# Linear attention with a two-layer SMELU feed-forward: loads put in an order, and scores, intra part and state moved to zero-padded weights

## The chip, the cores and the metric

The kernel runs on one core of one Trainium2 chip. The metric is the device time of one execution in microseconds (us). Several executions of each kernel are timed in the same rounds on the same chip, and each is marked fast or slow; only fast ones are compared. A profile's "span" is the time from its first to its last instruction. It is somewhat shorter than the reported time: 286.2 us against 287.86 us in the profiled execution of the changed kernel.

Engines are named as in the profile: PE is the matrix engine and PEld its weight load, DVE the vector engine, ACT the scalar engine, POOL the third elementwise engine (it also issues the weight loads here), SP the engine that issues most other transfers.

## The reference, cut to what matters

```python
# q, k, v: (4, 8, 768, 64) fp32, lam: (8,); w_in: (512, 2048), w_out: (2048, 512)
for b in range(nb):                                    # blocks of the sequence
    intra = einsum('bhic,bhjc->bhij', qb, kb) * Dmask  # lam^(i-j), lower triangle
    intra = einsum('bhij,bhjd->bhid', intra, vb)
    inter = einsum('bhid,bhde->bhie', qb * lam_pow, kv_state)
    out[:, :, sl] = intra + inter
    kv_state = lam_block * kv_state + einsum('bhsd,bhse->bhde', kb * rev_pow, vb)
x = out.transpose(0, 2, 1, 3).reshape(3072, 512)
h = x @ w_in
g = where(h >= 1, h, where(h <= -1, 0, (h + 1) ** 2 / 4))
return g @ w_out                                       # (3072, 512) fp32
```

The kernel cuts the 3072 tokens into 24 chunks of 128 (6 per batch entry). A chunk is done in two *units* of four heads, so there are 48 units. Four chunks make a *tile* of 512 tokens for the feed-forward layers; there are 6 tiles.

## The kernel before: the parts that matter

Each unit has three stages. `t` transposes q and multiplies k with [v | identity], which gives the state's update and k^T at once. `s` makes the scores, `o` the output of the chunk.

```python
def cast(c, k_eng):                      # fp32 to bf16, times lam^(+-position)
    nc.gpsimd.tensor_tensor(qs, qf, tab_q, mult)       # POOL
    k_eng.tensor_tensor(ks, kf, tab_k, mult)           # DVE for chunks 0-3, then POOL
    nc.scalar.copy(out=vi[c % NV][:, :, 0, :], in_=vf) # ACT; vi = [v | identity]

def stage_t(u):
    # 2 x transpose(pq <- qs), 2 x matmul(pk <- ks as weights, vi as rhs: 256 columns)
    for hi in range(2):
        nc.scalar.copy(out=qbd[u % NQ][hi*64:hi*64+64, :, hi, :], in_=pq[hi*64:hi*64+64])
    nc.scalar.copy(out=kT, in_=pk[:, :, 1, :])
    # U = pk[:, :, 0, :] + U of the chunk before                      (DVE)

def stage_s(u):
    for j in range(2):                   # q is block-diagonal and MOVES: 256 columns
        nc.tensor.matmul(ps[:, 2*j:2*j+2, :], lhsT=kT[:, j, :], rhs=qbd[u % NQ][:, j])
    # sc = ps * causal                                                (DVE)

def stage_o(u):
    for j in range(2):                   # 256 columns each
        # if not the first chunk: po[:, j] += U x qbd
        nc.tensor.matmul(po[:, j], lhsT=vi[..., hp, 0, :], rhs=sc[:, 2*j:2*j+2, :])
    # two ACT copies of 64 partitions put the diagonal blocks of po into xT

def att(i):                              # the order of the attention steps
    u, odd = i // 2, i % 2
    if not odd: ...                      # stage_t(u), and behind it stage_o(u - 1)
    else: ...                            # stage_s(u)
```

The order of the program is the order on each engine:

```python
load(0); load(1) ...                     # q, k, v of a chunk, 256 KB each
for c in range(4):                       # chunks 0 to 3
    cast(c)
    if c >= 1: load_w_in(...)            # weights between the chunks
    # four steps: t(2c), o(2c-1), s(2c), t(2c+1), o(2c), s(2c+1)
load_w_in(...); 4 x load_w_out(...)
ensure_cast(4); # one step: t(8), o(7)
for s in range(NST + 1):                 # then every group of layer 1 and layer 2
    for i in range(FO):                  # has an attention step woven into it
        ensure_loaded(c + 5); ensure_cast(c + 1)
        l1(s, i); todo_a(); smelu(s, i); l2(s - 1, i); todo_b()
```

In layer 1, ACT makes `r` = relu(`ph` + 1), and DVE makes from it `t` = min(r/2, 1), `w` = r - t and `gT` = w x t, the activated input of layer 2.

So chunks 4 to 8 are already worked on during layer 1 of the first tile, and the casts of a chunk are issued one chunk ahead.

Of the kernel before, what the change touches and what calls it, by code (L numbers as in the profile page):

```python
# [23 lines left out]
def kernel(  # L24
# [30 lines left out]
    NU = NCH * 2  # L55

    const = ctx.enter_context(tc.tile_pool(name="const", bufs=1))
    big = ctx.enter_context(tc.tile_pool(name="big", bufs=1))
    ld = ctx.enter_context(tc.tile_pool(name="ld", bufs=6))
    qkp = ctx.enter_context(tc.tile_pool(name="qkp", bufs=3))  # L60
    ktp = ctx.enter_context(tc.tile_pool(name="ktp", bufs=3))
    scp = ctx.enter_context(tc.tile_pool(name="scp", bufs=2))
    up = ctx.enter_context(tc.tile_pool(name="up", bufs=3))
# [15 lines left out]
    qkv_ld = {}  # L79

    def load(c):
        b, s0 = c // NCB, (c % NCB) * C
        ts = []
        for name, src in (("q", q), ("k", k), ("v", v)):
            t = ld.tile([128, H, D], F32, name=f"{name}f", tag=f"{name}f")
            nc.sync.dma_start(out=t, in_=src[b, :, s0:s0 + C, :].rearrange("h p d -> p h d"))
            ts.append(t)
        qkv_ld[c] = ts

    lam_b = const.tile([128, H], F32)  # L90
    nc.sync.dma_start(out=lam_b, in_=lam.partition_broadcast(128))
# [26 lines left out]
    NQ = 3  # L118
    qbd = []
    for i in range(NQ):  # L120
        t = const.tile([128, 2, 2, 128], BF16, name=f"qbd{i}")
        nc.vector.memset(t, 0.0)
        qbd.append(t)
    NV = 3
    vi = []
    for i in range(NV):
        t = const.tile([128, HP, 2, 128], BF16, name=f"vi{i}")
        nc.vector.tensor_copy(t[:, :, 1, :], _bc(ident, 1, HP))
        vi.append(t)

# [7 lines left out]
    def load_w_in(i):  # L138
        n = d_ff // WS
        nc.gpsimd.dma_start(out=w_in_sb[:, :, i * n:(i + 1) * n], in_=w_in_r[:, :, i * n:(i + 1) * n])  # L140

    def load_w_out(i):
        n = FO // WS
        nc.gpsimd.dma_start(out=w_out_sb[:, i * n:(i + 1) * n, :], in_=w_out_r[:, i * n:(i + 1) * n, :])
# [4 lines left out]
    def cast(c, k_eng):  # L149
        qf, kf, vf = qkv_ld.pop(c)  # L150
        cb = c % NCB
        t = qkp.tile([128, H, D], BF16, name="qs", tag="qs")
        nc.gpsimd.tensor_tensor(t, qf, _bc(tab_q[:, cb, :], 2, D), op=AX.mult)  # L153
        qs[c] = t
        t = qkp.tile([128, H, D], BF16, name="ks", tag="ks")
        k_eng.tensor_tensor(t, kf, _bc(tab_k[:, cb, :], 2, D), op=AX.mult)  # L156
        ks[c] = t
        nc.scalar.copy(out=vi[c % NV][:, :, 0, :], in_=vf.rearrange("p (a b) d -> p a (b d)", b=2))  # L158

    kT, U, sc_sb, xT = {}, {}, {}, {}  # L160

    def stage_t(u):
        c, hf = u // 2, u % 2
        cb = c % NCB
        pq = pp_q.tile([128, 2, 128], BF16, name="pq", tag="pq")
        pk = pp_k.tile([128, 2, 2, 128], F32, name="pk", tag="pk")
        for j in range(2):
            hp = 2 * hf + j
            nc.tensor.transpose(out=pq[:, j, :], in_=qs[c][:, 2 * hp:2 * hp + 2, :].rearrange("p a d -> p (a d)"),  # L169
                                identity=ident)  # L170
        for j in range(2):
            hp = 2 * hf + j
            nc.tensor.matmul(pk[:, j], lhsT=ks[c][:, 2 * hp:2 * hp + 2, :].rearrange("p a d -> p (a d)"),  # L173
                             rhs=vi[c % NV][:, hp], start=True, stop=True)
        qb = qbd[u % NQ]
        for hi in range(2):
            nc.scalar.copy(out=qb[hi * 64:hi * 64 + 64, :, hi, :], in_=pq[hi * 64:hi * 64 + 64])  # L177
        t = ktp.tile([128, 2, 128], BF16, name="kT", tag="kT")
        nc.scalar.copy(out=t, in_=pk[:, :, 1, :])  # L179
        kT[u] = t  # L180
        if cb < NCB - 1:
            t = up.tile([128, 2, 128], BF16, name="U", tag=f"U{hf}")
            if cb == 0:
                nc.vector.tensor_copy(t, pk[:, :, 0, :])
            else:
                nc.vector.tensor_tensor(t, pk[:, :, 0, :], U[u - 2], op=AX.add)  # L186
            U[u] = t

    def stage_s(u):
        ps = pp_s.tile([128, 4, 128], F32, name="ps", tag="ps")  # L190
        for j in range(2):
            nc.tensor.matmul(ps[:, 2 * j:2 * j + 2, :], lhsT=kT[u][:, j, :], rhs=qbd[u % NQ][:, j],  # L192
                             start=True, stop=True)
        t = scp.tile([128, 4, 128], BF16, name="sc", tag="sc")
        nc.vector.tensor_tensor(t, ps, _bc(causal, 1, 4), op=AX.mult)  # L195
        sc_sb[u] = t

    def stage_o(u):
        c, hf = u // 2, u % 2
        cb = c % NCB  # L200
        st, off = c // CPS, (c % CPS) * C
        po = pp_o.tile([128, 2, 2, 128], F32, name="po", tag="po")
        for j in range(2):
            hp = 2 * hf + j
            if cb > 0:
                nc.tensor.matmul(po[:, j], lhsT=U[u - 2][:, j, :], rhs=qbd[u % NQ][:, j], start=True, stop=False)  # L206
            nc.tensor.matmul(po[:, j], lhsT=vi[c % NV][:, hp, 0, :], rhs=sc_sb[u][:, 2 * j:2 * j + 2, :],  # L207
                             start=(cb == 0), stop=True)
        if st not in xT:
            xT[st] = xp.tile([128, KO, MS], BF16, name="xT", tag="xT")  # L210
        for hi in range(2):
            nc.scalar.copy(out=xT[st][hi * 64:hi * 64 + 64, 2 * hf:2 * hf + 2, off:off + C],  # L212
                           in_=po[hi * 64:hi * 64 + 64, :, hi, :])

    def att(i):

        u, odd = i // 2, i % 2
        a, b_ = [], []
        if not odd:
            if u < NU:  # L220
                a.append(lambda: stage_t(u))
            if 1 <= u <= NU:
                b_.append(lambda: stage_o(u - 1))
        elif u < NU:
            a.append(lambda: stage_s(u))
        return a, b_
# [4 lines left out]
    def l1(s, ni):  # L231
        ph = pp_h.tile([128, MS], F32, name="ph", tag="ph")
        for ko in range(KO):
            nc.tensor.matmul(ph, lhsT=w_in_sb[:, ko, ni * 128:(ni + 1) * 128], rhs=xT[s][:, ko, :],  # L234
                             start=(ko == 0), stop=(ko == KO - 1))
        if ni % 2 == 0:
            r_t[s] = rp.tile([128, 2, MS], BF16, name="r", tag="r")
        nc.scalar.activation(out=r_t[s][:, ni % 2, :], in_=ph, func=AF.Relu, bias=one[:, 0:1])  # L238

    def smelu(s, ni):  # L240
        if ni % 2 == 0:
            return
        r = r_t[s]
        if ni == 1:
# [5 lines left out]
        nc.vector.tensor_tensor(gT[s][:, ni - 1:ni + 1, :], w, t, op=AX.mult)  # L250
# [16 lines left out]
    PF = 5  # L267
    state = {"ld": 2, "cast": 0, "att": 0, "wi": 0, "wo": 0}

    def ensure_loaded(c):  # L270
        while state["ld"] <= min(c, NCH - 1):
            load(state["ld"])
            state["ld"] += 1

    def ensure_cast(c, k_eng=None):
        while state["cast"] <= min(c, NCH - 1):
            cast(state["cast"], k_eng or nc.gpsimd)
            state["cast"] += 1

    def att_step():  # L280
        a, b_ = att(state["att"])
        state["att"] += 1
        return a, b_

    NSUB = 2 * NU + 1


    ensure_loaded(CPS - 1)
    for c in range(CPS):
        ensure_cast(c, nc.vector)  # L290
        if c >= 1:
            load_w_in(state["wi"])
            state["wi"] += 1
        for _ in range(4):
            a, b_ = att_step()
            for f in a + b_:
                f()
    load_w_in(state["wi"])
    for i in range(WS):
        load_w_out(i)  # L300
    ensure_loaded(CPS + 1)
    ensure_cast(CPS)
    a, b_ = att_step()
    for f in a + b_:
        f()
    ensure_loaded(CPS + PF)

    def target(g):

        base = 4 * CPS + 1  # L310
        if g < 16:
            return base + (18 * (g + 1)) // 16
        return min(NSUB, base + 18 + (g - 15))

    for s in range(NST + 1):
        for i in range(FO):
            g = s * FO + i
            todo_a, todo_b = [], []
            while state["att"] < min(NSUB, target(g)):
                c = state["att"] // 4  # L320
                ensure_loaded(c + PF)
                ensure_cast(c + 1)
                a, b_ = att_step()
                todo_a += a
                todo_b += b_
            if s < NST:
                l1(s, i)
            for f in todo_a:
                f()
            if s < NST:  # L330
                smelu(s, i)
            if s > 0:
                l2(s - 1, i)
            for f in todo_b:
                f()
# [30 lines left out]
```

## Time and profile before

| what | before | where it is read |
|---|---|---|
| time | 263.87 us median (263.35 to 264.07, 4 runs) | runs |
| first layer-1 matmul (`ph`) | 43.19 us | timeline |
| first layer-2 matmul (`py`) | 79.10 us | timeline |
| PE idle before the first `py` | 35.6 of 79.1 us | windows |
| PE idle after it | 5.1 of 184.4 us | windows |
| 512-column matmul at full clock | 0.217 us | timeline |

The windows view of the kernel before, cut at its first `py`. Columns: stretch, its length, then for each engine the busy time with the number of instructions, the granted PE clock, the DMA share and GB/s.

```profile
0.00:79.10 79.10, 43.49 (x234) 23.83 (x237) 40.58 (x68) 49.77 (x119) 29.36 (x37) 0.89 1.17 203
79.10:263.50 184.40, 179.31 (x978) 94.84 (x995) 103.21 (x178) 123.94 (x270) 24.87 (x24) 0.99 0.29 73
```

The first number after a comma is PE. After 79.1 us PE is busy nearly without a break: from there on only fewer or faster matmuls help. Before it, PE is idle for 35.6 us. (23 of the 1232 matmul records are missing from this trace, so these sums are a little low.) The waits of PE in the kernel before say on what (engine, line, releaser: us in total, times, longest):

```profile
PE pk L173 <- ACT vi_152 L158: 12.6, 1, 12.6
PE pq L169 <- POOL qs L153: 6.7, 1, 6.7
PE ps L192 <- ACT kT L179: 5.0, 8, 1.9
PE po L207 <- DVE sc L195: 2.6, 2, 2.4
```

The one long wait is for the v cast of chunk 4, and the page says that ACT waited for the load itself there (11.9 us).

The timeline of PE before, an ordinary unit at 120 us (start, length, engine, line, what; lines of DVE, PEld and others left out):

```profile
120.33 0.28 PE L169 MATMUL pq<-ident,qs 128*128 128x128 bf16 x2
120.44 0.38 PE L173 MATMUL pk<-vi_152,ks 128*128 128x256 bf16 x2
120.66 1.03 PE L258 MATMUL py<-w_out_sb,gT 128*128 128x512 bf16 x4
...
121.12 0.74 ACT L177 COPY qbd_144<-pq 64x256 bf16<-64x256 bf16 x2
...
121.89 0.37 ACT L179 CAST kT<-pk 128x256 bf16<-128x256 f32 x1
121.96 1.03 PE L234 MATMUL ph<-xT,w_in_sb 128*128 128x512 bf16 x4
...
122.83 0.38 PE L192 MATMUL ps<-qbd_144,kT 128*128 128x256 bf16 x2
```

Between `pk` and `ps` stand a `py` group, an `o` stage and a `ph` group. That is time for all three ACT copies; PE does not wait. Starts give the cost of the matmuls: the four `py` matmuls start at 120.66 and what follows them starts at 121.53, so 0.217 us each; the two transposes take 0.11 us, or 0.055 us each. The Trainium skill (TensorE: Matmul & The Clock Gate, "Wait — 56ns, not 53.3ns?") gives 215.7 and 55.6 ns for back-to-back matmuls of 512 and 128 columns at full clock, and this trace agrees.

### The profile page before, as it was taken

What the parts mean: (1) busy time and instruction counts of PE and PEld (TensorE: products, weight loads), DVE (VectorE), ACT (ScalarE), POOL (GpSimd) and SP (SyncE); (2) the same over time, 40 slices, a digit from 0 to 9 for tenths busy, and PEclk for the clock granted to TensorE, in tenths of its full rate; (3) what the DMA queues carried; (4) which work ended last, traced back from release to release, by engine and by line L of the source; (5) the groups of instructions that cost most, each with busy time, mean ns of one, the idle gap of its engine ahead of it and who ended that gap; (6) DMA issues with size and microseconds to landing.
All of it is one profiled execution on the core that took longest, in us unless ns stands there. A gap on an engine that the chain in (4) does not pass through costs nothing.

```text
span 263.5 us, 3576 instructions
## 1 busy us (share of the span) xinstructions
PE 222.8 (85%) x1209; PEld 118.7 (45%) x1232; DVE 143.8 (55%) x245; ACT 173.7 (66%) x389; POOL 54.2 (21%) x61
## 2 busy tenths in 40 slices
PE   0567306666889999999999999999999999999993
PEld 0234203333445555555555555555555544444441
DVE  3554201388887576657574766574747645555300
ACT  4768303778996977797779777977796754554210
POOL 3418111552340332033303320333000000000000
PEclk9999755999999999999999999999999999999998
DMA  6999999999990526753574357110111011111122
GB/s 134 210 217 187 196 196 220 210 226 218 218 202 2 138 67 120 159 128 85 108 159 121 88 113 163 40 40 0 42 41 40 2 40 40 40 42 40 40 80 80
DMA packets 82721, 29.58 MB, mean 112 GB/s; under 512 B 75536, under 2 KB 79632, under 8 KB 82704
## 3 DMA queue, kind: packets, MB, share of 16 engines
q1 hardware_dynamic: 78480, 25.18, 45.5%
q0 software_dynamic: 4224, 4.19, 9.7%
q8 instruction: 9, 0.15, 0.3%
q14 instruction: 8, 0.07, 0.1%
HBM read 27.27 MB, written 6.29 MB: 127 GB/s over the span
## 4 chain that ended last, share of the span: by engine, by line
PE 69%; DVE 3%; ACT 1%; issue 0%; ACTq 0%
PE py L258 31%; PE ph L234 26%; PE po L207 3%; PE ps L192 3%; PE pk L173 2%; PE po L206 2%; PE pq L169 1%; DVE gT L250 1%; DVE w_726 L249 1%; DVE sc L195 0%; DVE w_768 L249 0%; ACT r L238 0%; DVE U L186 0%; ACT xT L212 0%; ACT osb L262 0%
## 5 line engine op out<-in xcount | busy, mean ns | idle before, releaser
L234 PE MATMUL ph<-xT,w_in_sb 128*128 128x512 bf16 x380 | 99.6, 383 | 1.7 <-ACT r L238 1.3
L238 ACT ACTIVATE r<-ph,one 128x512 bf16<-128x512 f32 x96 | 65.9, 687 | 43.3 <-PE ph L234 39.6
L258 PE MATMUL py<-w_out_sb,gT 128*128 128x512 bf16 x365 | 92.3, 379 | 1.0
L234 PEld LDWEIGHTS <-w_in_sb 128*128 128x128 bf16 x384 | 37.9, 99 | 37.6 <-issue 2.8
L258 PEld LDWEIGHTS <-gT 128*128 128x128 bf16 x384 | 37.6, 98 | 32.3
L153 POOL TENSOR_TENSOR qs<-qf,tab_q 128x512 bf16<-128x512 f32 x24 | 25.3, 1052 | 121.7 <-PE pq L169 92.0
L186 DVE TENSOR_TENSOR U<-pk,U 128x256 bf16<-128x256 f32 x32 | 13.6, 424 | 56.5 <-ACT kT L179 56.5
L212 ACT CAST xT<-po 64x256 bf16<-64x256 f32 x96 | 35.3, 367 | 4.5 <-PE po L207 3.7
L195 DVE TENSOR_TENSOR sc<-ps,causal 128x512 bf16<-128x512 f32 x48 | 32.9, 685 | 4.6 <-PE ps L192 4.0
L156 POOL TENSOR_TENSOR ks<-kf,tab_k 128x512 bf16<-128x512 f32 x20 | 22.3, 1117 | 7.9 <-DMA kf<-in_k_dram 7.9
L262 ACT COPY osb<-py 128x512 f32<-128x512 f32 x24 | 14.2, 591 | 12.4 <-PE py L258 12.4
L169 PE MATMUL pq<-ident,qs 128*128 128x128 bf16 x96 | 14.3, 235 | 6.7 <-POOL qs L153 6.7
L179 ACT CAST kT<-pk 128x256 bf16<-128x256 f32 x48 | 17.9, 372 | 2.4 <-PE pk L173 1.3
L173 PE MATMUL pk<-vi_152,ks 128*128 128x256 bf16 x32 | 6.8, 298 | 14.6 <-ACT vi_152 L158 12.6
L169 PEld LDWEIGHTS <-qs 128*128 128x128 bf16 x96 | 10.1, 106 | 16.8 <-POOL qs L153 6.7
L173 PEld LDWEIGHTS <-ks 128*128 128x128 bf16 x96 | 8.1, 103 | 20.5 <-issue 8.1
L192 PEld LDWEIGHTS <-kT 128*128 128x128 bf16 x96 | 8.5, 101 | 19.4 <-ACT kT L179 11.0
L158 ACT CAST vi_152<-vf 128x512 bf16<-128x512 f32 x8 | 4.9, 610 | 11.9 <-DMA vf<-in_v_dram 11.9
L177 ACT COPY qbd_146<-pq 64x256 bf16<-64x256 bf16 x32 | 11.6, 361 | 1.6 <-PE pq L169 1.2
L177 ACT COPY qbd_144<-pq 64x256 bf16<-64x256 bf16 x32 | 11.5, 361 | 0.6 <-PE pq L169 0.2
L177 ACT COPY qbd_148<-pq 64x256 bf16<-64x256 bf16 x32 | 11.5, 361 | 0.5
L206 PEld LDWEIGHTS <-U 128*128 128x128 bf16 x80 | 8.2, 102 | 7.8 <-issue 3.7
(187 smaller groups left out, 213.9 us busy)
## 6 DMA issues: line engine op xcount, KB each, us to landing
qf<-in_q_dram SPq DMA_DIRECT2D x24, 256.0 KB, 4.8
kf<-in_k_dram SPq DMA_DIRECT2D x24, 256.0 KB, 4.7
vf<-in_v_dram SPq DMA_DIRECT2D x24, 256.0 KB, 5.0
out_dram<-osb SPq DMA_DIRECT2D x24, 256.0 KB, 2.0
w_in_sb<-in_moe_w_in_dram POOLq DMA_DIRECT2D x4, 512.0 KB, 8.7
w_out_sb<-in_moe_w_out_dram POOLq DMA_DIRECT2D x4, 512.0 KB, 15.5
lam_b<-in_lam_dram SPq DMA_DIRECT2D x1, 4.0 KB, 2.9
```

Source lines behind the costliest of these rows:

```text
L153: nc.gpsimd.tensor_tensor(t, qf, _bc(tab_q[:, cb, :], 2, D), op=AX.mult)
L156: k_eng.tensor_tensor(t, kf, _bc(tab_k[:, cb, :], 2, D), op=AX.mult)
L169: nc.tensor.transpose(out=pq[:, j, :], in_=qs[c][:, 2 * hp:2 * hp + 2, :].rearrange("p a d -> p (a d)"), identity=ident)
L173: nc.tensor.matmul(pk[:, j], lhsT=ks[c][:, 2 * hp:2 * hp + 2, :].rearrange("p a d -> p (a d)"), rhs=vi[c % NV][:, hp], start=True, stop=True)
L177: nc.scalar.copy(out=qb[hi * 64:hi * 64 + 64, :, hi, :], in_=pq[hi * 64:hi * 64 + 64])
L179: nc.scalar.copy(out=t, in_=pk[:, :, 1, :])
L192: nc.tensor.matmul(ps[:, 2 * j:2 * j + 2, :], lhsT=kT[u][:, j, :], rhs=qbd[u % NQ][:, j], start=True, stop=True)
L195: nc.vector.tensor_tensor(t, ps, _bc(causal, 1, 4), op=AX.mult)
L212: nc.scalar.copy(out=xT[st][hi * 64:hi * 64 + 64, 2 * hf:2 * hf + 2, off:off + C], in_=po[hi * 64:hi * 64 + 64, :, hi, :])
L234: nc.tensor.matmul(ph, lhsT=w_in_sb[:, ko, ni * 128:(ni + 1) * 128], rhs=xT[s][:, ko, :], start=(ko == 0), stop=(ko == KO - 1))
L238: nc.scalar.activation(out=r_t[s][:, ni % 2, :], in_=ph, func=AF.Relu, bias=one[:, 0:1])
L258: nc.tensor.matmul(py, lhsT=gT[s][:, ko, ms * 128:(ms + 1) * 128], rhs=w_out_sb[:, ko, :], start=(ko == 0), stop=(ko == FO - 1))
```

## The change

The intent is twofold.

*Form.* Instead of moving a half-empty block-diagonal q (256 columns), k^T and v are made zero-padded *weights*, and q^T moves as it is (128 columns). In `s` four full-array matmuls of 128 columns replace two of 256. In `o` the state matmul moves 128 columns instead of 256, and the intra matmuls accumulate both heads into one output, so one ACT copy replaces two. The state is kept in block-diagonal tiles of 128 columns. The padding must be cleared once at the start.

*Order.* Chunks 0 to 3 are loaded first, then `w_in`, then chunks 4 to 7 (held back by a wait), then `w_out`, then the rest. The work follows that order.

```diff
-    for i in range(NQ): qbd[i] = const.tile([128, 2, 2, 128]); memset(0)
-    NV = 3;  vi[i] = [128, HP, 2, 128]; identity copied into [:, :, 1, :]
+    for i in range(NKB): kbd[i] = const.tile([128, 2, 2, 128]); memset(0)
+    for ...:             ubd[hf][i] = const.tile([128, 2, 128]); memset(0)
+    NV = 4;  vi[i] = [128, HP + 1, 2, 2, D]; memset(0), two identity copies
 ... stage_t
-        for hi: nc.scalar.copy(out=qb[64 rows, :, hi, :], in_=pq[64 rows])
-        nc.scalar.copy(out=kT, in_=pk[:, :, 1, :])
+        for hi: nc.scalar.copy(out=kb[r, :, hi, :], in_=pk[r, :, 1, :])
+        nc.scalar.copy(out=qT, in_=pq)
 ... stage_s
-            nc.tensor.matmul(ps[:, 2*j:2*j+2, :], lhsT=kT[u][:, j, :], rhs=qbd[u % NQ][:, j])
+            for hi in range(2):
+                nc.tensor.matmul(ps[:, 2*j+hi, :], lhsT=kbd[u % NKB][:, j, hi, :], rhs=qT[u][:, j, :])
 ... stage_o: the same for vi and ubd; one xT copy instead of two
 ... the order
+    for u in range(NU):                            # order of the attention steps
+        if u % 2 == 0 and u > 0: items += [("o", u - 1), ("t", u)]
+        else: items += [("t", u)] + ([("o", u - 1)] if u > 0 else [])
+        items.append(("s", u))
+    for c in range(CPS):
+        cast_to(c)
+        if c == CPS - 1:
+            4 x load_w_in; load_to(4, after=w_dma[2]); load_to(7)
+        att_to(done(c))                            # each chunk to its end
+    run(zip_(l1s(0, 1, 0), []), 0)                 # layer 1 of tile 0, nothing beside it
+    att_to(done(4))                                # chunk 4 alone
+    for c in range(5, 8):                          # chunks 5-7 beside layer 1 of tile 1,
+        run(zip_(l1s(1, CPS, c - CPS - 1), []), done(c) - st["it"])   # by quarters
+    4 x load_w_out; load_to(8, after=w_dma[6]); load_to(13); st["ahead"] = True
+    run(zip_(l1s(1, CPS, CPS - 1), []), 0)
+    run(zip_([], l2s(0)), done(11) - st["it"])
+    for s in range(2, NST + 1): ...                # layer 1 of s, layer 2 of s-1, 4 chunks
```

A *quarter* is layer 1 for the 128 tokens of one chunk, so its matmuls have 128 columns instead of 512.

Some small edits ride along. ACT's table is loaded once ahead instead of twice (1.28 us each), and `lam` is loaded from ACT's queue. There are 4 instead of 3 buffers for `vi` and for the cast q and k.

Only after `st["ahead"] = True` are casts issued before the chunk ahead of them is done.

## The prediction

> **What bounds it now.** The chain of waits is 69% PE. By windows, PE is busy 9.95 of every 10 us from 80 to 250 us; before that only 6.4 to 8.5, and nothing in 30 to 40 us, where the waits list shows pk <- vi (v cast) 12.6 us, vi <- v chunk 11.9 us. First py at 79.1 us. In the timeline at 120 us a 512-column matmul costs 0.217 us, a 256-column one 0.108, a transpose (128) 0.055. So PE work is about 211 us (768 x 0.217, and 48 half-chunk units of 0.97), and 52 of 263.5 us are stalls, nearly all early.
>
> **Removed.** Per unit the moving columns fall from 2304 to 2048: 0.97 to 0.88 us, 4 us in all, 3 of them in the PE-bound stage. This supposes 55 ns for a 128-column matmul with its own weights, which the transposes show only in pairs; the Trainium skill (TensorE: Matmul & The Clock Gate, "Back-to-back issue gap") gives about 81 ns sustained. ACT: 1.83 to 1.48 us per unit. One of two 1.28 us table loads. Weights no longer compete with chunks 0 to 3, so the 12.6 us wait goes; loads land by about 57 us (estimate from 215 and 196 GB/s in windows).
>
> **Added, by the order of instructions.**
> 1. DVE clears before the first ks: 3x256, 6x128, 4x640 words (0.27 us per 256 now) and copies, about 5.4 us. First pk at about 11 us (8.0 now).
> 2. Chunks 0 to 3 run one by one: the v cast of chunk c stands on ACT behind the last xT of c-1, and both kbd copies wait for pk. From the trace's pieces (cold pk pair 0.6, three ACT copies 1.13, ps 0.6, sc 0.69, po 0.8, xT 0.37, v cast 0.62) I get 7.4 us per chunk, longer than its load (3.7 us). Layer 1 starts at about 40 us (43.2 now), with chunk 4 not done.
> 3. Layer 1 of tile 0 runs alone (16 us), then chunk 4 alone (7 us), then chunks 5 to 7 beside the quarter-wise layer 1: pk waits for r and the v cast, the last o for sc without cover: about 9 us each where PE has 5.2. Layer 2 starts at about 94 us.
> 4. In every later chunk t and s of a unit are one matmul group (0.87 us) apart; s needs about 1.6 us (pk 0.38, three copies 1.13): 0.5 us of stall, 0.1 at the last o. During layer 2 of tile 0 nothing stands between: 1.4 us. Together 4 x 1.5 + 12 x 0.6 = 13 us. Before, 1.73 us stood between.
>
> **Sum.** From 94 us: layer 2 of tile 0 with four chunks 27, three tiles of 37, 28, 14, end 3.5: 277 us. Some early stalls may be shorter (full clock, faster clears): 271 us, slower by 3%, range 255 to 283. Chances: faster 0.2, same 0.22, slower 0.58.
>
> **What would show it.** Waits: pk <- ACT v cast and ps <- ACT qT, some 1 us each, dozens of times; DMA waits small after 20 us. Windows: PE at 25 to 45% in 10 to 40 us, about 75% in layer 2 of tile 0, 93 to 95% after (now 99.5%). First ph at 38 to 42 us, first py at 88 to 98.
>
> **What would make it wrong.** If chunks 0 to 3 take 5 us each and chunks 5 to 7 take 7, layer 2 starts at 78 us and the time is 255 to 260. If sustained 128-column matmuls cost 81 ns, it adds up to 20 us. If the copies finish sooner, step 4 vanishes.

## The result, and the profile after

Ratios in this document are the mean time of one kernel's fast runs over that of the kernel before in the same rounds, with a 95% interval; so they are not quite the ratio of the quoted medians.

The changed kernel takes 288.00 us (median of 4, 287.81 to 289.56) against 263.87 us: ratio 1.0931 (1.0890 to 1.0972), clearly slower. The direction was predicted, the size was not: 288.00 us lies above the range of 255 to 283 us.

| what | before | after |
|---|---|---|
| first `pk` | 8.02 us | 11.09 us |
| first `ph` | 43.19 us | 39.44 us |
| first `py` | 79.10 us | 100.23 us |
| PE idle before the first `py` | 35.6 us | 37.0 us |
| PE idle after it | 5.1 us | 15.2 us |

The windows of the changed kernel, cut at its first `py`, and the phases before it: chunks 0 to 3, layer 1 of tile 0, chunk 4, chunks 5 to 7 with the four quarters.

```profile
0.00:100.23 100.23, 63.20 (x537) 45.97 (x537) 57.66 (x116) 49.92 (x107) 28.87 (x37) 0.90 0.89 158
100.23:286.20 185.97, 170.79 (x1083) 90.02 (x1080) 100.38 (x185) 109.21 (x234) 32.41 (x24) 1.00 0.29 74
...
8.00:40.00 32.00, 16.57 (x108) 11.68 (x109) 15.52 (x36) 12.94 (x35) 11.64 (x12) 1.00 1.21 199
39.44:55.20 15.76, 15.76 (x66) 6.53 (x65) 11.36 (x19) 10.59 (x16) 6.75 (x8) 1.00 0.90 153
55.20:63.00 7.80, 3.73 (x29) 2.60 (x28) 5.88 (x12) 3.78 (x10) 2.08 (x2) 0.76 1.12 218
63.00:100.20 37.20, 27.28 (x339) 25.27 (x337) 21.33 (x34) 20.42 (x43) 6.68 (x6) 0.78 0.56 111
```

Two things are to be seen. After the first `py` PE is now idle for 15.2 us instead of 5.1. And the first `py` comes 21.1 us later. Part of that is only moved: layer 1 of tile 1 is now finished before it (64 x 0.217 = 13.9 us), which the kernel before does later. But the later stretch is not shorter by those 13.9 us; it takes 186.0 us against 184.4. (It also holds most of chunk 8, which the kernel before has done by its first `py`; at about 0.9 us of PE per unit that is under 2 us, an estimate from the unit times above.)

A caution about the clock column: from 10 to 40 us it reads 1.00, while two 256-column `pk` matmuls take 0.63 us there (timeline) as against 0.38 us at 120 us above. The durations show that PE ran at a lower speed; the column shows it only later (0.53 in 60 to 70 us).

The waits of PE after:

```profile
PE ps L222 <- ACT qT L207: 18.4, 26, 1.3
PE po L239 <- DVE sc L225: 8.9, 9, 2.5
PE pq L196 <- POOL qs L180: 6.1, 1, 6.1
PE pk L200 <- DVE ks L183: 4.6, 1, 4.6
```

The 12.6 us wait for a load is gone. In its place are 26 waits of `ps` for the last ACT copy, nine of `po` for the masked scores, and 4.6 us for the first `ks`, in front of which DVE clears the padded tiles.

How the 26 arise shows in the timeline of chunk 1:

```profile
17.69 0.62 ACT L185 CAST vi_164<-vf 128x512 bf16<-128x512 f32 x1
...
18.36 0.58 PE L200 MATMUL pk<-vi_164,ks 128*128 128x256 bf16 x2 [0.77 <-ACT vi_164 L185]
18.98 0.76 ACT L205 CAST kbd_146<-pk 64x256 bf16<-64x256 f32 x2 [0.67 <-PE pk L200]
19.77 0.37 ACT L207 COPY qT<-pq 128x256 bf16<-128x256 bf16 x1
...
20.19 0.58 PE L222 MATMUL ps<-qT,kbd_146 128*128 128x128 bf16 x4 [1.24 <-ACT qT L207]
```

In the old form `ps` needed one copy that reads `pk` (k^T); the two copies of q^T read `pq` and could run before `pk` was there (first unit: `pk` at 8.02, `ps` at 9.08 us). In the new form the two padded copies read `pk`, and the copy of q^T, which reads only `pq`, is issued behind them, so all three ACT copies (0.76 + 0.37 us) stand between `pk` and `ps` of a unit: 18.36 to 20.19 us. Nothing else is given to PE in that time. The third copy need not stand there: ACT was idle for 0.67 us before the padded copies, with `pq` done. No run here issues it first; its length of 0.37 us is an estimate of what that might take out of such a wait.

The middle phase, chunk 6, is best seen on three engines at once:

```profile
77.01 0.58 PE L200 MATMUL pk<-vi_168,ks 128*128 128x256 bf16 x2 [1.17 <-ACT vi_168 L185]
77.39 1.91 PE L254 MATMUL ph<-xT,w_in_sb 128*128 128x128 bf16 x16
...
79.76 0.69 DVE L225 TENSOR_TENSOR sc<-ps,causal 128x512 bf16<-128x512 f32 x1 [0.70 <-PE ps L222]
...
80.02 1.04 POOL L180 TENSOR_TENSOR qs<-qf,tab_q 128x512 bf16<-128x512 f32 x1 [8.06 <-PE pq L196]
80.37 0.98 DVE L271 TENSOR_SCALAR t_857<-r 128x1024 bf16<-128x1024 bf16 x1
81.02 1.23 POOL L183 TENSOR_TENSOR ks<-kf,tab_k 128x512 bf16<-128x512 f32 x1
81.06 1.06 PE L254 MATMUL ph<-xT,w_in_sb 128*128 128x128 bf16 x16
81.38 1.41 DVE L273 TENSOR_TENSOR w_859<-r,t_857 128x1024 bf16<-128x1024 bf16 x1
...
82.83 0.69 DVE L274 TENSOR_TENSOR gT<-w_859,t_857 128x1024 bf16<-128x1024 bf16 x1
...
84.06 0.69 DVE L225 TENSOR_TENSOR sc<-ps,causal 128x512 bf16<-128x512 f32 x1
...
84.67 0.42 DVE L271 TENSOR_SCALAR t_924<-r 128x1024 bf16<-128x1024 bf16 x1
84.81 0.40 PE L239 MATMUL po<-sc,vi_168 128*128 128x128 bf16 x4 [2.47 <-DVE sc L225]
85.12 0.69 DVE L273 TENSOR_TENSOR w_926<-r,t_924 128x1024 bf16<-128x1024 bf16 x1
```

The same sixteen 128-column matmuls take 1.91 us at 77.39 and 1.06 us at 81.06: PE's clock falls to half here and comes back. And DVE's `t` and `w` take 0.98 and 1.41 us while POOL is casting, but 0.42 and 0.69 us when it is not. The second `sc` of the chunk (84.06 us) stands behind them, and the last `po` waits 2.47 us.

The Trainium skill has both. It says (TensorE: Matmul & The Clock Gate, "A second HAM failure mode: psum-queue depth-cycling") of one measured kernel that frequent short idle times between groups of matmuls made its clock swing between half and full; here no wait in this phase is over 2.5 us, and the granted clock is 0.78 on average. It says (GPSIMD Engine Reference, "Key points") that POOL shares its memory interfaces with DVE and contends with DVE instructions that use two ports or two inputs in SBUF; here `w`, with two such inputs, goes from 0.69 to 1.41 us, while `sc`, which has one input in PSUM, stays at 0.68 to 0.69 us in all 48 instances. Whether this phase's 11 us per chunk come from these two is put to the test below.

### The profile page after: what moved, and what is told of

Read it like the earlier page. It is cut to its first block, busy times and chain, and to the rows that moved or that the text cites. A ratio compares the mean times of both kernels' runs of the same rounds, so it can differ in the third digit from the quotient of the medians.

```text
span 286.2 us, 4402 instructions
## 1 busy us (share of the span) xinstructions
PE 234.0 (82%) x1616; PEld 136.0 (48%) x1616; DVE 158.0 (55%) x300; ACT 159.1 (56%) x340; POOL 61.3 (21%) x61
## 5 line engine op out<-in xcount | busy, mean ns | idle before, releaser
L254 PE MATMUL ph<-xT,w_in_sb 128*128 128x512 bf16 (+1 forms) x576 | 103.7, 323 | 1.9 <-ACT xT L243 1.9
L284 PE MATMUL py<-w_out_sb,gT 128*128 128x512 bf16 x384 | 95.9, 379 | 0.0
L254 PEld LDWEIGHTS <-w_in_sb 128*128 128x128 bf16 x576 | 49.8, 105 | 32.0 <-issue 6.7
L180 POOL TENSOR_TENSOR qs<-qf,tab_q 128x512 bf16<-128x512 f32 x24 | 29.3, 1222 | 138.4 <-PE pq L196 95.1
L243 ACT CAST xT<-po 128x256 bf16<-128x256 f32 x48 | 18.1, 376 | 17.4 <-PE po L239 17.2
L183 POOL TENSOR_TENSOR ks<-kf,tab_k 128x512 bf16<-128x512 f32 x20 | 25.2, 1261 | 1.2 <-DMA kf<-in_k_dram 0.8
L205 ACT CAST kbd_142<-pk 64x256 bf16<-64x256 f32 x32 | 11.7, 367 | 18.3 <-PE pk L200 17.9
L205 ACT CAST kbd_146<-pk 64x256 bf16<-64x256 f32 x32 | 11.7, 367 | 14.4 <-PE pk L200 14.0
L205 ACT CAST kbd_144<-pk 64x256 bf16<-64x256 f32 x32 | 11.7, 367 | 13.9 <-PE pk L200 13.5
L207 ACT COPY qT<-pq 128x256 bf16<-128x256 bf16 x48 | 17.9, 373 | 1.2
L216 DVE TENSOR_TENSOR ubd_0_152<-pk,ubd_0_148 64x128 bf16<-64x128 f32 x16 | 4.6, 288 | 14.7 <-ACT kbd_146 L205 12.9
L222 PE MATMUL ps<-qT,kbd_142 128*128 128x128 bf16 x64 | 7.2, 244 | 6.4 <-ACT qT L207 6.3
L222 PE MATMUL ps<-qT,kbd_144 128*128 128x128 bf16 x64 | 7.0, 239 | 6.4 <-ACT qT L207 6.3
L222 PE MATMUL ps<-qT,kbd_146 128*128 128x128 bf16 x64 | 6.8, 234 | 6.0 <-ACT qT L207 5.8
```

Source lines behind the costliest of these rows:

```text
L180: nc.gpsimd.tensor_tensor(t, qf, _bc(tab_q[:, cb, :], 2, D), op=AX.mult)
L183: (nc.vector if c < CPS else nc.gpsimd).tensor_tensor(t, kf, _bc(tab_k[:, cb, :], 2, D), op=AX.mult)
L205: nc.scalar.copy(out=kb[r, :, hi, :], in_=pk[r, :, 1, :])
L207: nc.scalar.copy(out=t, in_=pq)
L222: nc.tensor.matmul(ps[:, 2 * j + hi, :], lhsT=kbd[u % NKB][:, j, hi, :], rhs=qT[u][:, j, :], start=True, stop=True)
L243: nc.scalar.copy(out=xT[sx][:, 2 * hf:2 * hf + 2, off:off + C], in_=po)
```

## The experiments

Times are medians of the fast runs among 4 each (the profiled one and three rounds), beside runs of the kernel before; all outputs were correct. The kernels of this section were timed in four batches on four chips, after the change itself; the medians of the kernel before lie within 0.6 us of each other (263.27 to 263.87), so differences between batches are good to about that.

### 1. The form alone, and the order alone

Theory A says that the order of instructions loses the time; a rival says that the padded form itself is slower (more matmuls and clears, and perhaps 128-column matmuls that cost more than 55 ns).

```diff
 # e1_form: the kernel before (its loads, its order, its casts), with the change's
-    qbd, vi, kT, U; stage_t, stage_s, stage_o of before
+    kbd, ubd, vi (all cleared at the start); stage_t, stage_s, stage_o of the change
```

> Loads and order of before, attention stages of the change (zero-padded k^T and v, block-diagonal state, their clears). My theory (the order costs, the form does not): 258 to 267 us, about 261: 3 us less matmul time in the PE-bound stage, clears hidden behind the loads. Rival (the form costs: 128-column matmuls with a weight load each, longer way from pk to scores): 275 us or more.

```diff
 # e2_order: the changed kernel (its loads, its order), with before's form
-    kbd, ubd, vi; stage_t, stage_s, stage_o of the change
+    qbd, vi (4 buffers), kT, U; stage_t, stage_s, stage_o of before
```

> Loads and order of the change, attention stages of before. My theory: most of the loss stays, 272 to 283 us, about 277; a part goes because scores wait for one copy after pk instead of three and the clears are shorter. Rival (the form costs): 266 us or less.

| kernel | time, us | ratio to before | first `ph` | first `py` |
|---|---|---|---|---|
| e1_form | 260.12 | 0.9862 (0.9813 to 0.9910) | 41.61 | 76.82 |
| e2_order | 283.97 | 1.0761 (1.0697 to 1.0825) | 33.62 | 97.10 |
| the change | 288.00 | 1.0931 (1.0890 to 1.0972) | 39.44 | 100.23 |

A window of e1_form behind its first `py`, and the waits of `ps` in e2_order:

```profile
80.00:100.00 20.00, 20.00 (x140) 11.09 (x138) 15.06 (x28) 13.86 (x32) 4.08 (x4) 1.00 0.49 107
...
PE ps L201 <- ACT kT L188: 9.4, 21, 1.4
```

The form alone gains 1.4%, 3.4 us, which is less than 2% but clear of the noise. In the profiles 2.6 us of the gain lie after the first `py` (181.8 us against 184.4), where the prediction gave 3 us for the saved columns. The rest lies in the part that waits for loads; the extra buffers may have a share in it, and it is not shown to come from the columns. The rival falls: in windows e1_form keeps PE busy all of the time from 80 to 240 us, and in the changed kernel sixteen 128-column matmuls, each with its own weights, go from 81.06 to 81.95 us, 0.056 us each.

The order alone loses 7.6%. Both together lose more than the sum: with the change's order the new form costs 4 us (283.97 to 288.00) where with the order before it gains 3.4. Two parts of this can be seen. One is the three-copy chain, which before's order covers (no wait of PE for a copy after e1_form's first `py`) and the change's does not: `ps` waits 9.4 us in 21 waits in e2_order and 18.4 us in 26 in the change. The other is the clears, which are part of the form: the first `pk` is at 7.80 us in e2_order and at 11.09 us in the change. How the 4 us divide is not shown; in the profiles 3.1 us of them are there by the first `py`. At 283.97 us e2_order lies just above its expected 272 to 283.

### 2. Each place of the order that loses

Four kernels mend one place each. First the clears: only the first `vi` tile is cleared before the first `ks`.

```diff
 # e3_clears: the changed kernel
-    for i in range(NV): ...; nc.vector.memset(t, 0.0); two identity copies
+    clear_vi(0)
 # in cast(c), behind ks:
+        if c + 1 < NV: clear_vi(c + 1)
```

> The change, but only the first v tile is cleared ahead of the first ks; the other three are cleared one per chunk later. Theory: first pk at about 8.0 us instead of 11.1 and everything after it moves with it: 285 us. Rival (the start is hidden behind loads): 288 us.

It took 286.46 us, ratio 1.0859 (1.0805 to 1.0912). The first `ph` came 2.9 us earlier (36.55 us), the first `py` only 1.2 us earlier (99.02 us). The rest was given back in layer 1 of tile 0 (0.8 us longer) and right behind it, where `pk` of chunk 4 waited 1.5 us for DVE instead of 0.5. The time fell by 1.5 us, half of the 3 us expected.

Next the cover in the later part: from chunk 8 on the steps are ordered t(u), o(u-1), s(u) for every unit.

```diff
 # e4_cover: the changed kernel, for u >= 16
-        if u % 2 == 0: o(u - 1), t(u), s(u)
+        t(u), o(u - 1), s(u)            # casts of the next chunk at t of the odd unit
```

> The change, but from chunk 8 on the output stage of the unit before stands between t and s of every unit, so that more matmuls lie between them (no added work). Theory: the waits of the scores for the q copy, 1.3 us in each of chunks 8 to 11 and 0.4 in each later one, nearly vanish: 279 us (276 to 282), PE above 98% busy from 165 to 240 us. Rival (these waits are hidden or only move): 286 to 288 us.

It took 278.62 us, ratio 1.0575 (1.0516 to 1.0635): 9.4 us less than the change. After its first `py` (100.35 us) the waits of `ps` for `qT` fell from 9.8 us in 16 waits to 1.8 us in 4. First the change, then e4_cover:

```profile
PE ps L222 <- ACT qT L207: 9.8, 16, 1.3
PE ps L222 <- ACT qT L207: 1.8, 4, 1.2
```

The prediction's step 4 is thereby shown: the idle time of 15.2 us after the first `py` is mostly this.

Then chunks 0 to 3: casts of the next chunk are issued ahead, and the steps are in the order t, o, s.

```diff
 # e5_ahead: the changed kernel, chunks 0 to 3
-        cast_to(c) when t(2c) is reached; o(u - 1), t(u), s(u)
+        cast_to(c + 1) right after t of the odd unit of c; t(u), o(u - 1), s(u)
```

> The change, but in chunks 0 to 3 the casts of chunk c+1 are issued before chunk c's last stages, and t(u+1) stands ahead of o(u). Theory: the 7.4 us per chunk fall to about 5 (two units of 2.45 us at half clock), layer 1 starts near 32 us instead of 39.4, and the time falls by about 7: 281 us (277 to 284). Rival (something later, such as the loads of chunks 4 to 7 landing at 44 us, catches the gain): 287 to 288.

It took 285.22 us, ratio 1.0827 (1.0809 to 1.0845), outside the 277 to 284 us expected. The period of a chunk fell from 7.4 to 5.4 us, nearly as expected, and the first `ph` came at 34.35 us, 5.1 us earlier. But the first `py` came only 2.7 us earlier. Layer 1 of tile 0 now ran beside POOL's casts of chunks 4 to 7 and was 0.7 us slower, with `t` at 1.26 and `gT` at 1.42 us; behind it `pk` of chunk 4 waited 2.2 us for DVE instead of 0.5. An early gain was half given back, as in e3_clears.

Last the middle: chunks 4 to 7 are woven into layer 1 of tile 0, and layer 1 of tile 1 runs whole.

```diff
 # e6_mid: the changed kernel
-    run(zip_(l1s(0, 1, 0), []), 0); att_to(done(4))
-    for c in range(5, 8): run(zip_(l1s(1, CPS, c - CPS - 1), []), done(c) - st["it"])
+    run(zip_(l1s(0, 1, 0), []), done(7) - st["it"])
-    run(zip_(l1s(1, CPS, CPS - 1), []), 0)
+    run(zip_(l1s(1, 1, 0), []), 0)
```

> The change, but attention of chunks 4 to 7 is spread over layer 1 of tile 0 and layer 1 of tile 1 runs whole, with 512 columns, ahead of layer 2. Theory: from layer 1's start at 39.4 us to the first layer 2 matmul takes about 48 us instead of 60.8: 275 us (271 to 279). Rival (work in that stage is bound by ACT, DVE or loads and only moves): 285 us or more.

It took 279.05 us, ratio 1.0585 (1.0558 to 1.0611): 9 us less than the change, just above what was expected. From the first `ph` (39.94) to the first `py` (92.55) it took 52.6 us instead of 60.8, not the 48 that were expected. Waits for the v cast of 1.2 us and of `po` for `sc` of up to 2.7 us remained: the weaving gives cover, but casts are still not issued ahead.

### 3. Why chunks 5 to 7 took 11 us each, not 9

The prediction gave 9 us per chunk in this phase. Two causes are in the trace: the half clock, and DVE stretched by POOL. Three kernels separate them.

```diff
 # e7_early_casts: the changed kernel; POOL no longer waits for buffers, and casts earlier
-    qkp = tc.tile_pool(name="qkp", bufs=4)
+    qkp = tc.tile_pool(name="qkp", bufs=8)
```

> The change with 8 instead of 4 buffers for the cast q and k, so that POOL casts chunks 9 to 11 when they land and not beside DVE's layer 1 work of chunks 5 to 7. If POOL's casts stretch DVE (w 1.41 us beside them, 0.69 without, in the trace) and this holds up the last o of chunks 5 to 7, these chunks fall from 11.0 to about 10 us each and the time to 285 to 286. If the lower PE clock alone made them 11 instead of my 9 us: 288, unchanged.

```diff
 # e8_fill: the changed kernel; PE's waits in chunks 1 to 7 are filled with matmuls
 # whose result is overwritten (no effect on the output)
+        for _ in range(10): nc.tensor.matmul(pk[:, 0, 1, :], lhsT=ks..., rhs=ident)  # before pk
+        for _ in range(...): nc.tensor.matmul(ps[:, 0, :], lhsT=ident, rhs=ident)    # before ps
+        for _ in range(...): nc.tensor.matmul(po[:, 0], lhsT=ident, rhs=ident)       # before po
```

> The change with extra matmuls of 128 columns put ahead of PE's waits in chunks 1 to 7; their results are overwritten. If PE's idle gaps keep its clock at half speed (chunk 0 to 3 and parts of 59 to 93 us) and that is a cause: matmuls of chunks 1 to 7 run at 0.055 us per 128 columns, chunks take 6.2 instead of 7.4 us, and the time falls by 5 to 10 to 278 to 283 although work is added. Rival (clock is not what holds these chunks; the chain of copies is): 288 or more.

```diff
 # e12_fill_casts: e7_early_casts and e8_fill together
```

> The change with both the filling matmuls of e8 and the 8 buffers of e7. My step 3 took 9 us for each of chunks 5 to 7, and they took 11. If the half clock and DVE work stretched by POOL casts are the two causes, then with both removed each of the three takes 8.8 to 9.3 us (e7's one chunk at full clock and without stretched w took 8.9) and the whole 281 to 282 us. Rival (the quarter-wise layer 1 has another cost that I missed): 10 us or more each, time as e8.

| kernel | time, us | ratio to before | chunks 5, 6, 7, us | first `py` |
|---|---|---|---|---|
| the change | 288.00 | 1.0931 (1.0890 to 1.0972) | 11.1, 10.9, 11.0 | 100.23 |
| e7_early_casts | 286.34 | 1.0874 (1.0858 to 1.0890) | 11.2, 8.9, 11.0 | 98.56 |
| e8_fill | 283.39 | 1.0765 (1.0742 to 1.0787) | 9.9, 10.2, 10.2 | 95.92 |
| e12_fill_casts | 281.15 | 1.0641 (1.0586 to 1.0696) | 8.6, 9.6, 9.0 | 92.02 |

In e7_early_casts chunk 6 had both the full clock and an unstretched `w`; it took 8.9 us, and chunks 5 and 7, which met the half clock again, took 11. Its timeline in chunk 6:

```profile
77.54 1.05 PE L254 MATMUL ph<-xT,w_in_sb 128*128 128x128 bf16 x16
...
80.48 0.69 DVE L273 TENSOR_TENSOR w<-r,t 128x1024 bf16<-128x1024 bf16 x1
...
83.18 0.40 PE L239 MATMUL po<-sc,vi 128*128 128x128 bf16 x4 [1.23 <-DVE sc L225]
```

In e8_fill PE kept its clock (all runs of sixteen in chunks 5 to 7 took 1.05 to 1.06 us) and a chunk took 10.1 us on average; `w` still took 1.41 us:

```profile
74.45 1.05 PE L264 MATMUL ph<-xT,w_in_sb 128*128 128x128 bf16 x16
...
77.91 1.41 DVE L283 TENSOR_TENSOR w<-r,t 128x1024 bf16<-128x1024 bf16 x1
...
81.32 0.38 PE L249 MATMUL po<-sc,vi 128*128 128x128 bf16 x4 [1.49 <-DVE sc L232]
```

With both, the three chunks took 9.1 us on average (60.59 to 87.85 us), the predicted 9; that is 1.0 us less per chunk than with the fill alone. The last `po` of chunk 6 waits 0.99 us there, although one `w` of that chunk still met a cast:

```profile
75.23 1.43 DVE L283 TENSOR_TENSOR w<-r,t 128x1024 bf16<-128x1024 bf16 x1
...
78.66 0.38 PE L249 MATMUL po<-sc,vi 128*128 128x128 bf16 x4 [0.99 <-DVE sc L232]
```

So the 2 us per chunk are settled as the work of these two together; the rival of 10 us or more is out, though single chunks (8.6 and 9.6 us) fall outside the 8.8 to 9.3 expected. The half clock costs about 0.9 us per chunk (e8_fill), DVE beside POOL about 1.0 us more once the clock is held (e12_fill_casts). This split depends on which is mended first: for the three chunks e7_early_casts alone saves 1.9 us, e8_fill alone 2.7 us, both 5.8 us; in chunk 5 of e7_early_casts PE ran at half clock for longer than in the change (two runs of sixteen at 1.9 us instead of one). That useless matmuls make the kernel 4.6 us faster is itself worth noting (278 to 283 us were expected, 283.39 measured): the fill also shortened chunks 2 and 3 (first `ph` at 37.17 us instead of 39.44).

### 4. A version that beats both

```diff
 # e9_best: the changed kernel (ordered loads, new form), and
+    t(u), o(u - 1), s(u) everywhere; casts one chunk ahead, except across the two load waits
+    clears as in e3_clears
+    chunks 4 to 7 woven into layer 1 of tile 0 from its fifth group on
+    chunks 8 to 11 woven into layer 1 of tile 1 and layer 2 of tile 0 from their fourth group on
```

> The change's loads and form with its order mended throughout: order t, o of the unit before, s; casts one chunk ahead; clears one chunk at a time; chunks 4 to 7 spread over layer 1 of tile 0 from its fifth group on, chunks 8 to 11 over layer 1 of tile 1 and layer 2 of tile 0. Theory (order was the loss, ordered loads and form are a gain): layer 1 starts at about 31 us, then about 201 us of matmul time at full clock, DVE-bound for some 5 us in tile 0, end 4: 241 us (236 to 250), faster than before. Rival (the ordered loads cost by themselves, since chunks 8 on land only after 60 us): 258 us or more.

It took 256.69 us (fast runs 256.15 to 257.07, one slow run of 261.08 left out), ratio 0.9725 (0.9655 to 0.9796): faster than the kernel before, but far from the 241 us expected and outside its range of 236 to 250. The first `ph` is at 31.14 us and the first `py` at 65.70 us. The waits of PE that are left in e9_best:

```profile
PE po L247 <- DVE sc L233: 9.5, 12, 1.5
PE pq L204 <- POOL qs L186: 6.0, 1, 6.0
PE ps L230 <- ACT qT L215: 5.5, 9, 1.3
```

`po` waits for DVE, which is busy 7.8 to 8.2 of every 10 us between 40 and 70 us. Two kernels tried to relieve it.

```diff
 # e10_best8: e9_best with early casts
-    qkp = tc.tile_pool(name="qkp", bufs=4)
+    qkp = tc.tile_pool(name="qkp", bufs=8)
```

> As e9 with 8 instead of 4 buffers for the cast q and k. If POOL casts that are held back by buffers and then fall beside DVE's work still cost, 1 to 3 us less than e9; otherwise the same.

```diff
 # e11_split: e9_best, one of the two kbd copies on DVE instead of ACT
-            nc.scalar.copy(out=kb[r, :, hi, :], in_=pk[r, :, 1, :])
+            (nc.scalar.copy if hi == 0 else nc.vector.tensor_copy)(out=..., in_=...)
```

> As e9 with one of the two k^T copies of each unit on DVE instead of ACT. If the chain pk, copies, scores still binds in chunks 0 to 3, they take about 0.4 us less per unit, 2 to 3 us in all; if DVE's load in tile 0 binds, it gets slower by as much.

Both were worse than e9_best: 260.32 us, ratio 0.9866 (0.9820 to 0.9911), and 259.28 us, ratio 0.9825 (0.9779 to 0.9872). In e10_best8, where 1 to 3 us less were expected, the waits of `po` for DVE rose from 9.5 to 11.7 us; in e11_split a new wait of `ps` for DVE's copy came up, 4.3 us. That fits DVE as the next limit in that stretch, but what e9_best still lacks to 241 us has not been taken apart.

Finally the loads. In e13_loads everything is as in e9_best, but the loads are in the order of the kernel before.

```diff
 # e13_loads: e9_best
-        if c == CPS - 1: 4 x load_w_in; load_to(4, after=w_dma[2]); load_to(7)
+        if c >= 1: load_w_in(c - 1)
+        if c == CPS - 1: load_w_in(c); 4 x load_w_out; load_to(7)
-    4 x load_w_out; load_to(8, after=w_dma[6])
```

> e9 with the loads issued as before: w_in between chunks 1 to 3, w_out right after, no load waits for another. If the ordered loads are a gain in a good order: 2 to 6 us slower than e9, 259 to 263 us, with a wait for chunk 5 near 30 to 40 us. If they gain nothing, or hold chunks 8 on back too long: 254 to 257.

It took 263.14 us, ratio 0.9973 (0.9917 to 1.0030). The wait for a late v load is back, 4.9 us in one piece, and the first `py` is at 71.30 us instead of 65.70:

```profile
PE pk L208 <- ACT vi L193: 6.0, 2, 4.9
```

So the ordered loads by themselves are good, worth about 6 us (263.14 to 256.69, in different rounds, by ratio 0.9973 to 0.9725) once the work is ordered to use them. In the change the wait for a load is gone as well, but the order of the work loses more than that.

## Why the prediction was right or wrong

The prediction's steps against the trace of the changed kernel:

| step | predicted | measured |
|---|---|---|
| first `pk`, behind the clears | 11 us | 11.09 us |
| period of chunks 0 to 3 | 7.4 us | 7.4 us |
| first `ph` | 40 us (38 to 42) | 39.44 us |
| layer 1 of tile 0 alone | 16 us | 15.8 us |
| chunk 4 alone | 7 us | 7.8 us |
| chunks 5 to 7 | about 9 us each | 11.1, 10.9, 11.0 us |
| first `py` | 94 us (88 to 98) | 100.23 us |
| layer 2 of tile 0 with four chunks | 27 us | 28.2 us |
| three tiles | 37 us each | 37.2 us each |
| tile 5, then the end | 28, then 17.5 us | 27.9, then 18.1 us |
| sum | 277 us | 286.2 us (span) |

**Right: what was removed.** Of "4 us in all, 3 of them in the PE-bound stage" e1_form shows 2.6 us in that stage (3.4 us in all). The assumption of 55 ns for a 128-column matmul with its own weights held. The Trainium skill's 81 ns (TensorE: Matmul & The Clock Gate, "Back-to-back issue gap"), which the prediction kept as a risk, by its estimate of up to 20 us, did not appear: sixteen of them from 81.06 us end where the next stage starts at 81.95 us, 0.056 us each. The wait of 12.6 us for a load went, as said.

**Right: that the order costs more than the loads gain, and where.** Clears, chunks one by one, a lone layer 1, a middle phase without cover and stalls in the later part were all found; e3_clears, e4_cover, e5_ahead and e6_mid each mend one place (e6_mid two), and each is faster than the change. Step 4 said 13 us of stalls after the first `py`; the trace shows 9.8 us of waits for `qT` there, and e4_cover wins 9.4 us by covering them. Of the windows that it named, PE was busy for 79% of layer 2 of tile 0 (75% predicted) and for 95% in the three tiles after (93 to 95%), but for 55% from 10 to 40 us (25 to 45%). The period of 7.4 us was met exactly, but the pieces listed for it add up to 4.8 us, and the prediction does not write how they become 7.4; how much of this hit is luck can't be checked.

**Wrong, first: the discount.** The sum was 277 us. The prediction then took 6 us off, "Some early stalls may be shorter (full clock, faster clears)". Nothing in the trace supported that: the clears took as long as costed, the chunks ran at half clock with a period of 7.4 us. PE's full clock, which the discount hoped for early, was instead lost once more in the middle.

**Wrong, second: step 3, "about 9 us each".** Chunks 5 to 7 took 11 us each, 6 us in all. The waits named there were the right ones (the v cast 1.1 to 1.2 us, the last `o` up to 2.47 us). What was left out are two couplings: with PE so often idle its clock fell to half (0.9 us per chunk by e8_fill), and POOL's casts, which in this order fall right on DVE's chain of layer 1, about doubled its `w` (1.0 us more per chunk by e12_fill_casts). With both removed the chunks take 9.1 us, the 9 that were predicted. So the mechanism was right and this term was mis-sized: 27 us predicted, 33 us measured.

**Wrong, smaller.** Chunk 4 took 0.8 us more and the layer-2 stage of tile 0 took 1.2 us more than costed. The reported time also holds 1.7 us outside the span (287.86 against 286.2), which the sum left out. The sum of 277 plus these terms (6 + 0.8 + 1.2 + 1.7, and 0.6 at the end) is 287.3 us, against 288.0 measured.

**Where the expected gain went.** The ordered loads removed a 12.6 us wait for chunk 4, but only the order of the work could have turned this into time. In the kernel before attention steps are woven into every group of layer 1, and from its first `py` on PE waits for no copy at all (before it, `ps` waits for `kT` 8 times, 5.0 us). In the change PE waits for the last copy 26 times, 18.4 us. And time saved early was often given back: e3_clears and e5_ahead reached the first `ph` 2.9 and 5.1 us sooner, and kept 1.2 and 2.7 us of it at the first `py`.

**Still open.** Why e9_best misses 241 us is read from windows only (DVE's load, early chunks without cover, a clock of 0.83 in 40 to 50 us); none of the three was tested by itself. And what share of idle time makes PE's clock fall is not settled: it stayed at 1.00 in the kernel before from 50 to 70 us, with PE busy 6.8 to 6.9 of 10 us, and was 0.83 in the change from 70 to 90 us with 6.0 to 6.8 of 10.

## What to carry to other kernels

An order of loads is only worth what the order of the work can take from it: judge the two apart, by running each with the other's old version. When a form of computation puts more copies between two matmuls of one unit, count what stands between them on PE, give PE another unit's work there, and ask which of the copies have to stand there at all. And when you sum a stage from the durations of its pieces, ask whether those durations hold there (here the same matmuls took 1.91 instead of 1.06 us where PE was often idle, and `w` 1.41 instead of 0.69 us beside POOL's casts), and take nothing off the sum that no line of the trace supports.

## What the Trainium skill lacked or had wrong

- TensorE: Matmul & The Clock Gate, "Back-to-back issue gap": its sustained figures of about 81 ns for 128 columns and 131 ns for 512 columns were not met. With a new weight tile for every matmul the runs show 0.056 us (sixteen between 81.06 and 81.95 us of the changed kernel) and 0.217 us. The figures that the same page has further up, 55.6 and 215.7 ns, are the ones that fit.
- The same page, "What's actually happening", has PE go to half clock after an idle window of about 3.4 us. Here matmuls went to half speed at 59.32 us of the changed kernel (two of 256 columns in 0.61 us, after 0.38 at 56.67) although PE had worked without a break from 39.44 to 55.23 us and its waits since then were 1.24 us at most; the page's remark on oscillation fits, but it gives no share of idle time from which it happens.
- GPSIMD Engine Reference, "Key points", names the contention of POOL and DVE without a size in that place (other pages of the skill say more of who waits; they were not used here). The runs show: `w`, two bf16 inputs in SBUF, 0.69 to 1.41 us; `t`, one input, 0.42 to 0.98 us; POOL's own cast of `ks` 1.04 to 1.49 us; `sc`, one input in PSUM, unchanged at 0.69 us.
- TensorE: Matmul & The Clock Gate, "Seeing it yourself", warns that recorded clock events can be unreliable, but does not say that they can show full clock while matmuls run slowly. Here the clock column reads 1.00 from 10 to 40 us of the changed kernel while two 256-column matmuls take 0.63 us, against 0.38 us where PE is busy all the time; durations are the safer witness.
